# Fixed adjacent pairs of PSUM banks for the exponentials, in place of a pool of single banks, with order rules per stretch to go with them

## The chip, the cores and the metric

One core of a Trainium2 chip. The metric is the device time of one execution in microseconds, the median of several runs; all runs quoted are of the undisturbed state or, for this one-core program, within 1.5% of the fastest of their kernel.

Engines: PE is the TensorE, ACT the ScalarE, DVE the VectorE, POOL the GpSimd.

## The reference, cut

```python
q = (xn @ wq).reshape(B, S, H, Dh)      # S 2048, D 640, H 32 heads of Dh 20
k, v = xn @ wk, xn @ wv                 # one key/value head for all
p = softmax(einsum("bhqd,bkd->bhqk", q, k) * Dh ** -0.5)
attn = einsum("bhqk,bkd->bhqd", p, v).reshape(B, S, H * Dh) @ wo
r = maximum(xn @ w1 + b1, 0)            # F 1536
out = x + attn + (r * r) @ w2 + b2      # xn = layernorm(x)
```

The scores are 32 x 2048 x 2048: 2048 tiles of 128 keys x 512 queries, each an exponential. Most go to ACT; the others are converted on DVE by a bit trick (a scaled integer read as bf16, four weighted copies of it standing for 2^x), in "sets" of four tiles.

## The kernel before

The Python program plans the whole execution first: a greedy planner holds one queue per engine and durations for each operation, picks the next instruction by start time and priority, and only then emits each engine's list with its semaphore waits. Parameters of the planner are overridden per 10 us by RULES. A change of a rule or a bank therefore moves thousands of instructions.

A score visit takes banks for an ACT instruction; this is the part that the change switches (cut):

```python
def make_step():
    j = len(steps)
    if par("STATIC"):
        banks = list(SIDES[j % 2])                  # (0, 1) or (2, 3)
        if any(bank_state(bk) is None for bk in banks):
            return None
        return build_step(j, banks, 0.0)
    t0 = max(free["PE"], horizon() - par("JIT"))
    st_of = {bk: bank_state(bk) for bk in range(NB)}     # NB = 7
    ok = [bk for bk in range(NB) if st_of[bk] is not None and st_of[bk] <= t0 + 0.02]
    if len(ok) >= 3 + par("R3"):                    # three tiles when banks are plenty
        ...
    # else the two adjacent banks that come free first
    ...
def pool_banks():                                   # for DVE tiles and dense units
    if par("STATIC"):
        return [bk for bk in POOLED if bk not in HELD and bank_state(bk) is not None]   # 4, 5, 6
    fb = [bk for bk in POOLED if bank_state(bk) is not None]
    return fb if len(fb) > par("KEEP") else []
```

When a visit is placed, DVE tiles of other heads ride along in it, because row-tiled matmuls of four heads run side by side: in the trace of the kernel before, a visit of two, three or four tiles takes 0.318, 0.321 or 0.325 us until the next group starts.

```python
elif kind == "qk":
    take_step(ap[1])
    heads = [t[2] for t in ap[1]["tiles"]]
    while len(heads) < HPG:                         # HPG = 4
        r = make_dqk(heads)
        ...
        commit(r[0])
        after_dqk(*r)
```

Nearly all other PE work (weighted values, query and key projections, the two dense layers, the output) is column-tiled in groups of four matmuls, most of 512 or 320 columns; the transposes and the value projection use the whole array (128*128 in the views). A unit of the dense layers is a run of such groups into one bank.

The softmax here doesn't subtract the row's maximum and nothing guards it: scores larger than these inputs give would overflow.

Of the kernel before, what the change touches and what calls it, by code (L numbers as in the profile page):

```python
# [24 lines left out]
SCALE = DH ** -0.5  # L25
EPS = 1e-5
EXP_SHIFT = 50.0
# [8 lines left out]
def _pl(z):  # L36
# [9 lines left out]
NB = 7  # L46
PVB = 7
SHARED = (4, 5, 6)
STATIC = False
SIDES = ((0, 1), (2, 3))  # L50
POOLED = tuple(range(NB))
HELD = sum(SIDES, ())
EVP = 0.8
JIT = 0.8
R3 = 2
NOPEN = 2
# [3 lines left out]
DRATE = 0.95  # L60
DLAST = 7.5
DSLACK = 0
URG = 4.0
PBIAS = 0.6
DGAP = 0.5
# [3 lines left out]
WARM = 0.72  # L69
# [7 lines left out]
STG = 10.0  # L77
TAIL0 = 2
ACTEV = (0, 2)
KEEP = 1  # L80
RULES = {3: {'PVA': 2.1, 'PVD': 2.1, 'R3': 1, 'PP': 0.9},
         4: {'PVA': 2.1, 'PVD': 2.1, 'R3': 1, 'PP': 0.9, 'WARM': 0.78},
         5: {'D1P': 1, 'MPRIO': 0.5, 'PBIAS': 2.5},
         6: {'D1P': 1, 'MPRIO': 0.5, 'PBIAS': 2.5, 'ND': 1, 'QKP': 0},
         7: {'DQP': 2.05, 'URG': 2, 'PVD': 2.1, 'BEHIND': -0.3},
         8: {'WARM': 0.85, 'DQP': 0.95},
         10: {'ND': 1, 'NOPEN': 3},
         11: {'ND': 1, 'NOPEN': 3},
         12: {'EPS': 0.12},
         13: {'EPS': 0.06, 'EVP': 0.3},  # L90
         15: {'PBIAS': 0},
         17: {'EPS': 0.06},
         18: {'EPS': 0.12},
         19: {'WARM': 0.78, 'PBIAS': 2.5, 'IDLE': 0.3},
         21: {'PBIAS': 0, 'KEEP': 0},
         23: {'EPS': 0.12},
         25: {'R3': 1, 'EVP': 0.3},
         26: {'R3': 1, 'EVP': 0.3, 'IDLE': 0.3, 'PVD': 2.1},
         28: {'EPS': 0.12, 'URG': 3},
         29: {'EPS': 0.12, 'URG': 3, 'KEEP': 3, 'EVP': 1.1, 'ND': 3},  # L100
         31: {'PBIAS': 1, 'D1P': 1, 'PVD': 1.05},
         32: {'PBIAS': 1, 'D1P': 1, 'PVD': 1.05, 'DGAP': 0.8, 'DQP': 0.95, 'SQP': 2, 'R3': 1},
         36: {'PP': 0.9, 'BEHIND': -0.1, 'EVP': 0.3, 'PBIAS': 1.5},
         37: {'URG': 3, 'JIT': 1.0, 'PVD': 1},
         38: {'SQP': 0.7, 'URG': 3},
         39: {'PP': 2.5},
         40: {'PBIAS': 1},
         41: {'PBIAS': 1, 'DGAP': 1.5, 'SQP': 0.7},
         42: {'PBIAS': 1, 'DGAP': 1.5, 'SQP': 2, 'NOPEN': 3, 'ND': 2, 'PVD': 1},
         43: {'PBIAS': 1, 'DGAP': 1.5, 'SQP': 2, 'NOPEN': 3, 'ND': 2, 'PVD': 1, 'R3': 9},  # L110
         44: {'WARM': 0.78, 'KEEP': 3, 'DLAST': 7.5},
         45: {'DGAP': 0.8, 'KEEP': 1, 'D1P': 3},
         48: {'PBIAS': 1},
         49: {'PBIAS': 1, 'R3': 1},
         50: {'PBIAS': 1, 'R3': 1},
         53: {'DLAST': 3.5},
         54: {'DLAST': 3.5, 'EPS': 0, 'EVP': 0.3},
         55: {'DLAST': 3.5, 'EPS': 0, 'EVP': 0.3, 'ND': 1},
         56: {'EVP': 2, 'MPRIO': 1.0},
         57: {'R3': 1, 'ND': 1},  # L120
         58: {'BEHIND': -0.1, 'EPS': 0, 'PP': 4, 'R3': 1},
         59: {'BEHIND': -0.1, 'EPS': 0, 'PP': 4, 'R3': 1, 'DRATE': 0.95, 'DLAST': 10, 'PVA': 2.1},
         60: {'EVP': 1.1},
         61: {'EVP': 1.1, 'SQP': 0.7},
         62: {'EVP': 1.1, 'SQP': 0.7, 'KEEP': 3, 'R3': 1, 'NOPEN': 2, 'D1P': 3},
         64: {'PP': 0.9, 'DRATE': 0.8},
         65: {'R3': 1},
         66: {'R3': 1},
         67: {'EPS': 0.12, 'PVA': 1.05},
         68: {'R3': 0},  # L130
         69: {'R3': 0, 'JIT': 1.1}}
HOOK = None
PRIO = {'NM15': 2.12, 'NM10': 2.88, 'PW2': 0.96}
NBEF = {'AG4': 10.21, 'NM7': 11.5, 'Qe0_1': 10.11, 'PW12': 25.33}
XACT = (1, 3)
QEACT = (0, 1, 2, 3)
STOP = None
WINDOW = 3.4
MPRIO = 0.9
BEHIND = 0.12  # L140
IDLE = 0.3
EARLY = 12
EARLYK = "F"
FFN0 = 0.3
OUT0 = 0.5
QLEAD = 3.0
PEND = NBLK - 3.0
QCPOS = 0
ACTST = (2, 5, 6)
POOLXN = (2, 7, 9, 10, 11, 13, 14, 15)  # L150
ROWP = (-0.5, 0.6, 0.8, 1.2)


# [3 lines left out]
MODEL = {}  # L157

DEFAULTS = dict(EVP=EVP, PBIAS=PBIAS, MPRIO=MPRIO, DGAP=DGAP, DLAST=DLAST, DRATE=DRATE, BEHIND=BEHIND, IDLE=IDLE, URG=URG, NOPEN=NOPEN,
                EPS=0.03, JIT=JIT, R3=R3, STATIC=STATIC, PVA=1, PVD=1, D1P=1, PP=4, SQP=2, DQP=3, QKP=0, ND=2, WARM=WARM, KEEP=KEEP)  # L160


class Ctr:
# [61 lines left out]
def bass_parallel_sum__grouped_kv_mqa__dense_activation_squared_relu__prompt_kernel(nc, A_x, A_wq, A_wk, A_wv, A_wo, B_x, B_w1, B_b1, B_w2, B_b2, out):  # L225
    es = ExitStack()
    with es:  # L227
# [71 lines left out]
        def one():  # L299
            nsem[0] += 1  # L300
            return newctr(f"d{nsem[0]}")
# [3 lines left out]
        free = {k: 0.0 for k in ENG}  # L305
# [36 lines left out]
        dve_q, pool_q, sp_q, act_q = [], [], [], []  # L342
# [3 lines left out]
        def op(name, eng, dur, fn, deps=(), **kw):  # L346
            o = Op(name, eng, dur, [fn], deps, **kw)
            o.prio = PRIO.get(name, o.prio)
            o.nb = NBEF.get(name, 0.0)
            ev = [d for d in o.deps if isinstance(d, str)]  # L350
            if ev:
                late.setdefault(ev[0], []).append(o)
            else:
                QUE[eng].append(o)
            return o
# [59 lines left out]
        def rows(st):  # L415

            p = ROWP[st // 4]
            if st in ACTST:
                k = ACTST.index(st)
                jk = OC[:, 0, :, :].rearrange("p c n -> p (c n)")[:, k * D:(k + 1) * D] if k < 4 else out_sb[:, k - 4, :]  # L420
# [4 lines left out]
            else:  # L425
# [4 lines left out]
                opm = ALU.subtract  # L430
                if st in POOLXN:
                    s1 = op(f"NM{st}", "DVE", 0.08, lambda e: e.tensor_scalar(out=mv[:, st, 0:1], in0=mv[:, st, 0:1], scalar1=-1.0, scalar2=None, op0=ALU.mult), [ag], prio=p - 0.1)
# [13 lines left out]
        def bank_state(bk):  # L446

            if bank_busy[bk]:
                return None
            o = bank_rel[bk]  # L450
            if o is not None and o.fin is None:
                return None
            return 0.0 if o is None else o.fin + LATS[(o.eng, "PE")]
# [19 lines left out]
        for st in range(4):  # L473
# [17 lines left out]
            k0_op[st] = op(f"KTe0_{st}", "DVE", 0.25, lambda e, cs=cs, kb=kb: e.tensor_scalar(out=kT[:, cs], in0=ps[:, kb, 0:128], scalar1=nk0[:, 1:2], scalar2=None, op0=ALU.add), [km, nk_op], prio=0)  # L491
            if st in QEACT:
                q0_op[st] = op(f"Qe0_{st}", "ACT", 0.25, lambda e, cs=cs, st=st: e.activation(out=qT[:, 0, cs], in_=ps[:, st, 0:128], func=AF.Identity), [qm])
# [24 lines left out]
        def need_k(kt):  # L518
            return [k0_op[kt]] if kt < 4 else [kt_op[kt // 4]]
# [230 lines left out]
        for st in range(0, ST, 2):  # L750
            r0, r1 = 128 * st, 128 * st + 256
            o = op(f"XB{st}", "POOL", 1.25, lambda e, r0=r0, r1=r1: e.dma_start(xbd[r0:r1, :], A_x[0][r0:r1, :], accum_op=ALU.add, max_dma_last_dim=4 * D),
                   [x_b2[st], x_b2[st + 1], HOLD["xb"][st // 2]], lat=12.0, dma=one(), prio=3)
# [22 lines left out]
        left = sum(cost(u) for u, _ in chain)  # L776
        others, t = [], FFN0
        for u, t0 in chain:
# [58 lines left out]
        def next_stage():  # L837
            while free["ACT"] >= stage[0] * STG:
# [3 lines left out]
                now_rules.clear()  # L842
                now_rules.update(RULES.get(stage[0], {}))

        def par(name):

            return now_rules.get(name, DEFAULTS[name])
# [5 lines that stand above are left out]
                banks = list(SIDES[j % 2])  # L853
# [187 lines left out]
        def pool_banks():  # L1041

            if par("STATIC"):
                return [bk for bk in POOLED if bk not in HELD and bank_state(bk) is not None]
            fb = [bk for bk in POOLED if bank_state(bk) is not None]
            return fb if len(fb) > par("KEEP") else []
# [5 lines left out]
        def make_dqk(heads):  # L1052
            opn = [s for s in sets[-NL:] if s["left"]]
            fb = pool_banks()
            if not fb or (len(fb) == 1 and behind()):
                return None
            s = next((s for s in opn if [h for h in s["left"] if h not in heads]), None)
            if s is None:
                if len(opn) >= par("NOPEN"):
                    return None  # L1060
                s = new_set()
                if s is None:
                    return None
            h = [h for h in s["left"] if h not in heads][0]
            b, kt = s["b"], s["kt"]
            deps = need_k(kt) + need_q(b)
            bank = pick_bank(fb)
            deps.append(bank_rel[bank])
            return Op(f"DQK{s['n']}_{h}", "PE", 0.215, [mm(ps[:, bank, :], kT[32 * h:32 * h + DH, kt * 128:(kt + 1) * 128], qT[32 * h:32 * h + DH, b % NQS, :], True, True, (32 * h, 0))],
                      deps, mode="R"), s, h, bank  # L1070
# [121 lines left out]
        while True:  # L1192
# [81 lines left out]
            if pick[2].eng == "PE" and unit[0] is None and fb and pick[0] > free["PE"] + par("IDLE") and pv_begun:  # L1274
                for u in misc[:EARLY]:
                    if u.at > progress() and u.name[0] in EARLYK and u.can():
# [3 lines left out]
                        o = Op(f"{u.name}.0", "PE", dur, ch(), list(u.deps()) + [bank_rel[u.bank]])  # L1280
# [15 lines left out]
            _, prio, o, ap = pick  # L1296
# [162 lines left out]
```

## Time and profile before

| | before |
|---|---|
| time, median | 705.43 us (3 runs), 705.88 with the fourth |
| span of the profile | 703.6 us |
| ACT instructions of exponentials | 665 of two tiles, 50 of three |
| DVE tiles | 568 = 142 sets |
| score visits of PE | 714 |

A "visit" is an unbroken run of score matmuls (out<-in `ps<-qT,kT`) on PE. The visits, and the distances from one start to the next, are counted from the trace; the page has no row for them. The rows that the argument starts from stand in the prediction.

### The profile page before, as it was taken

What the parts mean: (1) busy time and instruction counts of PE and PEld (TensorE: products, weight loads), DVE (VectorE), ACT (ScalarE), POOL (GpSimd) and SP (SyncE); (2) the same over time, 40 slices, a digit from 0 to 9 for tenths busy, and PEclk for the clock granted to TensorE, in tenths of its full rate; (3) what the DMA queues carried; (4) which work ended last, traced back from release to release, by engine and by line L of the source; (5) the groups of instructions that cost most, each with busy time, mean ns of one, the idle gap of its engine ahead of it and who ended that gap; (6) DMA issues with size and microseconds to landing.
All of it is one profiled execution on the core that took longest, in us unless ns stands there. A gap on an engine that the chain in (4) does not pass through costs nothing.

```text
span 703.6 us, 22608 instructions
## 1 busy us (share of the span) xinstructions
PE 695.0 (99%) x9780; PEld 216.0 (31%) x9781; DVE 645.9 (92%) x1125; ACT 687.5 (98%) x739; POOL 427.3 (61%) x268
## 2 busy tenths in 40 slices
PE   8999999999999999999999999999999999999997
PEld 4422223233322223332322222323333222233333
DVE  7789999999999998989998998899899999999894
ACT  6899999999999999999999999999999999999995
POOL 4767556567566764666568765766665675644253
PEclk9999999999999999999999999999999999999999
DMA  6325422233337701211101001111112100031201
GB/s 201 98 70 153 115 78 58 81 97 80 84 85 160 162 20 25 55 40 37 52 18 40 23 22 28 29 47 26 46 42 51 36 22 23 20 106 51 55 26 39
DMA packets 42016, 44.00 MB, mean 63 GB/s; under 512 B 15540, under 2 KB 32772, under 8 KB 41788
## 3 DMA queue, kind: packets, MB, share of 16 engines
q1 hardware_dynamic: 39132, 36.93, 19.2%
q0 software_dynamic: 2208, 5.25, 3.9%
q8 instruction: 76, 1.25, 0.7%
q10 hardware_dynamic: 576, 0.38, 0.2%
q14 instruction: 24, 0.20, 0.1%
HBM read 28.03 MB, written 14.91 MB: 61 GB/s over the span
## 4 chain that ended last, share of the span: by engine, by line
ACT 95%; PE 4%; DMA 1%; DVE 0%; SPq 0%; issue 0%; DVEq 0%
ACT PT L910 94%; PE ps L367 3%; DMA x_sb<-in_A_x_dram 1%; PE ps L540 1%; ACT xnT L477 0%; ACT OC L421 0%; DVE out_sb L1164 0%; PE ps L568 0%; SPq L384 0%; ACT OC L422 0%; SPq L391 0%; PE ps L510 0%; PE ps L496 0%; DVEq L227 0%; DVE PT L1164 0%
## 5 line engine op out<-in xcount | busy, mean ns | idle before, releaser
L910 ACT ACTIVATE PT<-ps 128x1024 bf16<-128x1024 f32 (+1 forms) x715 | 677.1, 1219 | 3.8 <-PE ps L367 3.8
L1083 DVE TENSOR_SCALAR tmore<-ps 128x512 uint16<-128x512 f32 x568 | 367.4, 683 | 31.7 <-PE ps L367 28.2
L1101 POOL TENSOR_SCALAR tmore<-tmore 128x2048 uint16<-128x2048 uint16 x109 | 206.4, 1900 | 171.1 <-PE ps L367 62.3
L367 PE MATMUL ps<-qT,kT 20*128 20x512 bf16 x2048 | 281.7, 384 | 1.9 <-ACT PT L910 0.8
L1101 POOL TENSOR_SCALAR x_sb<-tmore 128x2048 uint16<-128x2048 uint16 x100 | 189.3, 1902 | 79.4 <-DVE x_sb L1101 24.2
L367 PEld LDWEIGHTS ps<-qT,kT 20*128 20x128 bf16 x2048 | 71.6, 91 | 280.4 <-ACT PT L910 233.1
L367 PE MATMUL ps<-PT,vx 128*32 128x512 bf16 x1480 | 136.9, 386 | 0.2 <-ACT PT L910 0.2
L1101 DVE TENSOR_SCALAR x_sb<-tmore 128x2048 uint16<-128x2048 uint16 x135 | 96.1, 745 | 0.1
L367 PE MATMUL ps<-x_sb,vxs 128*32 128x512 bf16 x940 | 83.2, 382 | 0.0
L367 PE MATMUL ps<-xnT,w_sb 128*32 128x512 bf16 x960 | 77.2, 384 | 0.1
L367 PE MATMUL ps<-w_sb,big 128*32 128x320 bf16 x1536 | 74.5, 302 | 0.0
L367 PE MATMUL ps<-tmore,vxs 128*32 128x512 bf16 x764 | 69.6, 382 | 0.0
L1101 DVE TENSOR_SCALAR tmore<-tmore 128x2048 uint16<-128x2048 uint16 x82 | 61.5, 770 | 0.1
L367 PE MATMUL ps<-tmore,vx 128*32 128x512 bf16 x568 | 55.7, 382 | 0.0
L367 PEld LDWEIGHTS ps<-PT,vx 128*32 128x32 bf16 x1480 | 34.9, 94 | 62.1 <-issue 53.6
L367 PEld LDWEIGHTS ps<-w_sb,big 128*32 128x32 bf16 x1536 | 32.1, 95 | 29.3 <-issue 22.2
L648 DVE TENSOR_SCALAR hT_tmp<-ps,b1col 128x512 bf16<-128x512 f32 x48 | 35.8, 746 | 3.4 <-PE ps L367 2.7
L367 PE MATMUL ps<-xnT,wq_sb 128*32 128x512 bf16 (+1 forms) x480 | 33.7, 356 | 0.2 <-DVE tmore L1083 0.2
L367 PE MATMUL ps<-wo_c,OC 128*32 128x320 bf16 x608 | 30.9, 301 | 0.0
L367 PEld LDWEIGHTS ps<-x_sb,vxs 128*32 128x32 bf16 x940 | 21.3, 95 | 19.9 <-issue 13.4
L367 PEld LDWEIGHTS ps<-xnT,w_sb 128*32 128x32 bf16 x960 | 17.6, 94 | 26.7 <-issue 22.4
L367 PEld LDWEIGHTS ps<-tmore,vxs 128*32 128x32 bf16 x764 | 18.1, 95 | 16.4 <-issue 11.5
(81 smaller groups left out, 259.4 us busy)
## 6 DMA issues: line engine op xcount, KB each, us to landing
xbd<-b2d SPq DMA_DIRECT2D x16, 320.0 KB, 4.4
xbd<-in_A_x_dram POOLq DMA_DIRECT2D x8, 640.0 KB, 5.8
xr<-xbd SPq DMA_DIRECT2D x32, 160.0 KB, 2.4
w_sb<-in_B_w_dram SPq DMA_DIRECT2D x8, 480.0 KB, 4.4
big<-OR SPq DMA_DIRECT2D x71, 40.0 KB
big<-drs SPq DMA_DIRECT2D x71, 40.0 KB
out_dram<-out_sb SPq DMA_DIRECT2D x15, 160.0 KB, 1.8
qT<-QCr SPq DMA_DIRECT2D x108, 20.0 KB
```

The source lines that it names most:

```text
L367: return lambda e: e.matmul(out_, l, r, start=start, stop=stop, tile_position=tp)
L540: return [(lambda e, dt=dt: e.transpose(out=psbf(bk)[:, dt * 128:(dt + 1) * 128], in_=xn_sb[:, st, dt:D:DT], identity=ident[:])) for dt in ...
L648: o = Op(f"RL{qc}_{f}", "DVE", 0.66, [lambda e: e.tensor_scalar(out=hT_tmp[:, k % 2, :], in0=ps[:, bk, :], scalar1=b1col[:, f:f + 1], scal ...
L910: return Op(f"ACT{st_['j']}", "ACT", 0.05 + 0.4267 * n, [lambda e: e.activation(out=PT[:, s0:s0 + n, :], in_=ps[:, b0:b0 + (n - 1) * db + ...
L1083: d1 = op(f"D1_{n}_{i}", "DVE", 0.60, lambda e: e.tensor_scalar(out=L[:, cs].bitcast(U16), in0=ps[:, bank, :], scalar1=XA, scalar2=XB, op0 ...
L1101: p = op(f"P{j}_{n}", eng, 0.60 if eng == "DVE" else 1.86, lambda e, T=T, j=j, two=two: e.tensor_scalar(out=T.bitcast(U16), in0=L.bitcast( ...
```

## The change

The intent: give ACT two fixed sides that alternate, so that its supply no longer depends on what the pool has free, leave three banks to everybody else, and choose the rules of all 70 stretches anew for this layout. The durations that the planner uses are the same numbers in both files. The diff, cut:

```diff
-STATIC = False
+STATIC = True
 SIDES = ((0, 1), (2, 3))
...
-KEEP = 1
-RULES = {3: {'PVA': 2.1, 'PVD': 2.1, 'R3': 1, 'PP': 0.9},
...
-         69: {'R3': 0, 'JIT': 1.1}}
+KEEP = 0
+DJIT = 9.0
+RULES = {1: {'EPS': 0.12},
...
+         62: {'NOPEN': 1, 'DGAP': 0.5, 'URG': 3, 'PVD': 1, 'QKP': 1.5},
+         63: {'DGAP': 0, 'PVA': 1.05, 'URG': 2, 'PBIAS': 0},
+         64: {'DGAP': 0.25, 'PVA': 1.05, 'URG': 2, 'PBIAS': 0, 'ND': 3},
+         65: {'DGAP': 0.25, 'PVA': 1.05, 'URG': 2, 'PBIAS': 0, 'ND': 3, 'DQP': 3, 'QKP': 0.97},
...
-QEACT = (0, 1, 2, 3)
+QEACT = (0, 1)
...
-FFN0 = 0.3
+FFN0 = 0.6
...
-ACTST = (2, 5, 6)
-POOLXN = (2, 7, 9, 10, 11, 13, 14, 15)
+ACTST = (0, 2, 4)
+POOLXN = (7, 9, 10, 11, 13, 14, 15)
...
+            if max(free["DVE"], free["PE"]) + sum(o.dur for o in dve_q if o.frees is not None) > free["PE"] + 0.43 + par("DJIT"):
+                return None
```

QKP is the priority of a score visit on PE (lower goes first; 0 by default), MPRIO that of the next group of a dense unit (0.9 by default).

More of the change, by code (lines that the diff above doesn't have):

```diff
@@ L79 @@
 ACTEV = (0, 2)
-KEEP = 1
-RULES = {3: {'PVA': 2.1, 'PVD': 2.1, 'R3': 1, 'PP': 0.9},
-         4: {'PVA': 2.1, 'PVD': 2.1, 'R3': 1, 'PP': 0.9, 'WARM': 0.78},
-         5: {'D1P': 1, 'MPRIO': 0.5, 'PBIAS': 2.5},
-         6: {'D1P': 1, 'MPRIO': 0.5, 'PBIAS': 2.5, 'ND': 1, 'QKP': 0},
-         7: {'DQP': 2.05, 'URG': 2, 'PVD': 2.1, 'BEHIND': -0.3},
-         8: {'WARM': 0.85, 'DQP': 0.95},
-         10: {'ND': 1, 'NOPEN': 3},
-         11: {'ND': 1, 'NOPEN': 3},
-         12: {'EPS': 0.12},
-         13: {'EPS': 0.06, 'EVP': 0.3},
-         15: {'PBIAS': 0},
-         17: {'EPS': 0.06},
-         18: {'EPS': 0.12},
-         19: {'WARM': 0.78, 'PBIAS': 2.5, 'IDLE': 0.3},
-         21: {'PBIAS': 0, 'KEEP': 0},
-         23: {'EPS': 0.12},
-         25: {'R3': 1, 'EVP': 0.3},
-         26: {'R3': 1, 'EVP': 0.3, 'IDLE': 0.3, 'PVD': 2.1},
-         28: {'EPS': 0.12, 'URG': 3},
-         29: {'EPS': 0.12, 'URG': 3, 'KEEP': 3, 'EVP': 1.1, 'ND': 3},
-         31: {'PBIAS': 1, 'D1P': 1, 'PVD': 1.05},
-         32: {'PBIAS': 1, 'D1P': 1, 'PVD': 1.05, 'DGAP': 0.8, 'DQP': 0.95, 'SQP': 2, 'R3': 1},
-         36: {'PP': 0.9, 'BEHIND': -0.1, 'EVP': 0.3, 'PBIAS': 1.5},
-         37: {'URG': 3, 'JIT': 1.0, 'PVD': 1},
-         38: {'SQP': 0.7, 'URG': 3},
-         39: {'PP': 2.5},
-         40: {'PBIAS': 1},
-         41: {'PBIAS': 1, 'DGAP': 1.5, 'SQP': 0.7},
-         42: {'PBIAS': 1, 'DGAP': 1.5, 'SQP': 2, 'NOPEN': 3, 'ND': 2, 'PVD': 1},
-         43: {'PBIAS': 1, 'DGAP': 1.5, 'SQP': 2, 'NOPEN': 3, 'ND': 2, 'PVD': 1, 'R3': 9},
-         44: {'WARM': 0.78, 'KEEP': 3, 'DLAST': 7.5},
-         45: {'DGAP': 0.8, 'KEEP': 1, 'D1P': 3},
-         48: {'PBIAS': 1},
-         49: {'PBIAS': 1, 'R3': 1},
-         50: {'PBIAS': 1, 'R3': 1},
-         53: {'DLAST': 3.5},
-         54: {'DLAST': 3.5, 'EPS': 0, 'EVP': 0.3},
-         55: {'DLAST': 3.5, 'EPS': 0, 'EVP': 0.3, 'ND': 1},
-         56: {'EVP': 2, 'MPRIO': 1.0},
-         57: {'R3': 1, 'ND': 1},
-         58: {'BEHIND': -0.1, 'EPS': 0, 'PP': 4, 'R3': 1},
-         59: {'BEHIND': -0.1, 'EPS': 0, 'PP': 4, 'R3': 1, 'DRATE': 0.95, 'DLAST': 10, 'PVA': 2.1},
-         60: {'EVP': 1.1},
-         61: {'EVP': 1.1, 'SQP': 0.7},
-         62: {'EVP': 1.1, 'SQP': 0.7, 'KEEP': 3, 'R3': 1, 'NOPEN': 2, 'D1P': 3},
-         64: {'PP': 0.9, 'DRATE': 0.8},
-         65: {'R3': 1},
-         66: {'R3': 1},
-         67: {'EPS': 0.12, 'PVA': 1.05},
-         68: {'R3': 0},
-         69: {'R3': 0, 'JIT': 1.1}}
@@ new lines @@
+KEEP = 0
+DJIT = 9.0
+RULES = {1: {'EPS': 0.12},
+         2: {'DGAP': 0.8, 'QKP': 1.5},
+         3: {'DGAP': 0.8, 'QKP': 0.97},
+         5: {'DQP': 0.95, 'PBIAS': 1.5},
+         6: {'DQP': 0.95, 'PBIAS': 1.5},
+         7: {'DLAST': 4.5, 'SQP': 0.7, 'DRATE': 1.1, 'BEHIND': -0.3},
+         8: {'DLAST': 4.5, 'SQP': 0.7, 'DRATE': 1.1, 'BEHIND': -0.3},
+         10: {'PVD': 2.1},
+         12: {'PBIAS': 0.3, 'IDLE': 0.2, 'BEHIND': 0.05},
+         13: {'PBIAS': 0.3, 'IDLE': 0.2, 'BEHIND': 0.05, 'ND': 3, 'NOPEN': 3},
+         14: {'PBIAS': 0.3, 'IDLE': 0.2, 'BEHIND': 0.05, 'ND': 3, 'NOPEN': 3, 'DRATE': 0.8, 'EPS': 0.12},
+         16: {'EPS': 0.12},
+         17: {'PVD': 0.95},
+         19: {'DRATE': 0.8, 'EPS': 0.06},
+         20: {'DRATE': 0.8, 'EPS': 0.06, 'EVP': 0.3, 'MPRIO': 1.1},
+         22: {'WARM': 0.78, 'ND': 1, 'DRATE': 1.1},
+         25: {'PP': 2.5, 'SQP': 0.7, 'DQP': 3},
+         26: {'PBIAS': 0, 'WARM': 0.85, 'SQP': 0.7, 'PVD': 1.05},
+         27: {'PBIAS': 0, 'WARM': 0.85, 'SQP': 0.7, 'PVD': 1.05},
+         28: {'PBIAS': 2.5, 'WARM': 0.85, 'SQP': 0.7, 'PVD': 1.05, 'D1P': 3, 'URG': 3, 'EVP': 0.3},
+         29: {'PBIAS': 2.5, 'WARM': 0.85, 'SQP': 0.7, 'PVD': 1.05, 'D1P': 3, 'URG': 3, 'EVP': 0.3, 'IDLE': 0.1, 'EPS': 0.12, 'DLAST': 7.5},
+         30: {'DQP': 0.95, 'PBIAS': 0.6},
+         31: {'EPS': 0.06},
+         32: {'EPS': 0.06, 'DGAP': 0.5, 'D1P': 0.5, 'PP': 0.9},
+         34: {'DLAST': 3.5, 'DGAP': 0.5},
+         35: {'PP': 0.9, 'SQP': 2},
+         36: {'MPRIO': 0.9, 'PBIAS': 2.5, 'PVD': 1, 'DLAST': 7.5},
+         37: {'MPRIO': 0.9, 'PBIAS': 2.5, 'PVD': 1, 'DLAST': 3.5, 'EVP': 2, 'D1P': 3},
+         39: {'D1P': 1, 'SQP': 0.7, 'URG': 4, 'PBIAS': 2.5},
+         40: {'D1P': 1, 'SQP': 0.7, 'URG': 4, 'PBIAS': 2.5, 'NOPEN': 1},
+         41: {'ND': 1},
+         42: {'ND': 1, 'EPS': 0.12, 'SQP': 0.7, 'D1P': 1},
+         43: {'ND': 1, 'EPS': 0.12, 'SQP': 0.7, 'D1P': 1},
+         44: {'ND': 1, 'EPS': 0.12, 'SQP': 0.7, 'D1P': 1, 'PVA': 1.05, 'NOPEN': 2},
+         45: {'ND': 1, 'EPS': 0.12, 'SQP': 0.7, 'D1P': 1, 'PVA': 1.05, 'NOPEN': 2},
+         46: {'ND': 1, 'EPS': 0.06, 'SQP': 0.7, 'D1P': 1, 'PVA': 1.05, 'NOPEN': 2},
+         47: {'DRATE': 0.95, 'MPRIO': 0.5, 'WARM': 0.72, 'D1P': 0.5},
+         48: {'DRATE': 0.95, 'MPRIO': 0.5, 'WARM': 0.72, 'D1P': 0.5},
+         49: {'DRATE': 0.95, 'MPRIO': 0.5, 'WARM': 0.72, 'D1P': 0.5, 'ND': 1, 'DQP': 2.05},
+         51: {'PP': 2.5},
+         52: {'PP': 2.5, 'EPS': 0.06},
+         53: {'PP': 2.5, 'EPS': 0.06, 'D1P': 3, 'DRATE': 0.95},
+         54: {'PP': 2.5, 'EPS': 0.06, 'D1P': 3, 'DRATE': 0.95, 'MPRIO': 1.0, 'EVP': 1.1, 'PVA': 0.95, 'DQP': 0.95},
+         55: {'URG': 2, 'MPRIO': 1.0, 'QKP': 0.97},
+         58: {'PVA': 1.05},
+         59: {'DLAST': 8.5, 'WARM': 0.78, 'PP': 0.9},
+         60: {'NOPEN': 2, 'DGAP': 0.5, 'URG': 3},
+         61: {'NOPEN': 1, 'DGAP': 0.5, 'URG': 3, 'PVD': 1},
+         62: {'NOPEN': 1, 'DGAP': 0.5, 'URG': 3, 'PVD': 1, 'QKP': 1.5},
+         63: {'DGAP': 0, 'PVA': 1.05, 'URG': 2, 'PBIAS': 0},
+         64: {'DGAP': 0.25, 'PVA': 1.05, 'URG': 2, 'PBIAS': 0, 'ND': 3},
+         65: {'DGAP': 0.25, 'PVA': 1.05, 'URG': 2, 'PBIAS': 0, 'ND': 3, 'DQP': 3, 'QKP': 0.97},
+         68: {'DLAST': 5.5, 'MPRIO': 1.0},
+         69: {'DLAST': 5.5, 'MPRIO': 1.0},
+         70: {'QKP': 0.97, 'DQP': 3, 'MPRIO': 0.9}}
@@ L132 @@
 HOOK = None
-PRIO = {'NM15': 2.12, 'NM10': 2.88, 'PW2': 0.96}
-NBEF = {'AG4': 10.21, 'NM7': 11.5, 'Qe0_1': 10.11, 'PW12': 25.33}
+PRIO = {'XN1': 0.13}
+NBEF = {'S4a': 6.0, 'AG5': 10.23, 'PW1': 4.94}
 XACT = (1, 3)
-QEACT = (0, 1, 2, 3)
+QEACT = (0, 1)
 STOP = None
@@ L159 @@
 DEFAULTS = dict(EVP=EVP, PBIAS=PBIAS, MPRIO=MPRIO, DGAP=DGAP, DLAST=DLAST, DRATE=DRATE, BEHIND=BEHIND, IDLE=IDLE, URG=URG, NOPEN=NOPEN,
-                EPS=0.03, JIT=JIT, R3=R3, STATIC=STATIC, PVA=1, PVD=1, D1P=1, PP=4, SQP=2, DQP=3, QKP=0, ND=2, WARM=WARM, KEEP=KEEP)
+                EPS=0.03, JIT=JIT, R3=R3, STATIC=STATIC, PVA=1, PVD=1, D1P=1, PP=4, SQP=2, DQP=3, QKP=0, ND=2, WARM=WARM, KEEP=KEEP, DJIT=DJIT)
 class Ctr:
```

## The prediction

> **What bounds the kernel now.** First the head of the page and the chain of work that ended last.
>
> ```profile
> PE 695.0 (99%) x9780; PEld 216.0 (31%) x9781; DVE 645.9 (92%) x1125; ACT 687.5 (98%) x739; POOL 427.3 (61%) x268
> ...
> ACT 95%; PE 4%; DMA 1%; DVE 0%; SPq 0%; issue 0%; DVEq 0%
> ACT PT L910 94%; PE ps L367 3%; DMA x_sb<-in_A_x_dram 1%; PE ps L540 1%; ACT xnT L477 0%; ACT OC L421 0%; DVE out_sb L1164 0%; PE ps L568 0%; SPq L384 0%; ACT OC L422 0%; SPq L391 0%; PE ps L510 0%; PE ps L496 0%; DVEq L227 0%; DVE PT L1164 0%
> ```
>
> The chain says ScalarE (ACT): its exponentials (L910) fill 94% of the span. But PE is busy 99% too, so the chain, which follows one engine, does not settle which of the two is the limit. Next, the groups by shape: how the score tiles (128x512 each, 2048 in all) are shared out.
>
> ```profile
> L910 ACT ACTIVATE PT<-ps 128x1024 bf16<-128x1024 f32 x665 | 621.9, 1190 | 1.4 <-PE ps L367 1.4
> L910 ACT ACTIVATE PT<-ps 128x1536 bf16<-128x1536 f32 x50 | 79.0, 1609 | 2.3 <-PE ps L367 2.3
> ...
> L1083 DVE TENSOR_SCALAR tmore<-ps 128x512 uint16<-128x512 f32 x568 | 367.4, 683 | 31.7 <-PE ps L367 28.2
> ...
> L367 PE MATMUL ps<-qT,kT 20*128 20x512 bf16 x2048 | 281.7, 384 | 1.9 <-ACT PT L910 0.8
> ```
>
> 665x2 + 50x3 = 1480 tiles go through ACT in 715 instructions; 568 tiles go through VectorE (DVE), which is 142 sets of four. The mean durations (1190, 1609) overlap their neighbours, so I took start-to-start distances from the trace: a two-tile instruction follows at 0.904 us (its median and its tenth percentile), a three-tile one at 1.330. 665x0.904 + 50x1.330 = 667.7 us. The first starts at 15.30 and the last ends at 695.14, 679.8 later: 12 us more than the floor, of which 3 lie in two waits before 33 us (0.5 and 2.5) and some 8.6 are hundreds of delays too short to show as idle. After the last there are 8.5 us of tail.
>
> Now PE, in the timeline from 420 to 424 us:
>
> ```profile
> 420.77 0.61 PE L367 MATMUL ps<-xnT,wq_sb 128*32 128x512 bf16 x8
> ...
> 421.32 0.39 PE L367 MATMUL ps<-qT,kT 20*128 20x512 bf16 x3
> ...
> 421.64 0.40 PE L367 MATMUL ps<-xnT,wq_sb 128*32 128x512 bf16 x4
> ...
> 421.87 0.39 PE L367 MATMUL ps<-PT,vx 128*32 128x512 bf16 x4
> ...
> 422.19 0.39 PE L367 MATMUL ps<-qT,kT 20*128 20x512 bf16 x2
> 422.50 0.12 PEld L367 LDWEIGHTS ps<-xnT,w_sb 128*32 128x32 bf16 x8 [0.23 <-issue]
> 422.51 0.62 PE L367 MATMUL ps<-xnT,w_sb 128*32 128x512 bf16 x8
> ```
>
> The score matmuls split the array by rows, all others by columns. From scores to others the next start comes 0.32 us later, from others to others 0.22-0.23, from others back to scores 0.32. So a visit to the scores costs about 0.322 + 0.105 = 0.427 us, whether it makes two, three or four tiles. I grouped the trace's matmuls so: 714 visits for 715 ACT instructions, i.e. nearly every DVE tile rides along in a visit that ACT needs anyway. Set against these floors (0.216 and 0.321 for 512 columns, 0.136 and 0.241 for 320, 0.318 after scores), PE loses only 8.5 us to waits over 13 ns between 33 and 690 us. PE is therefore as full as ACT: two bounds at once, PE 1.3% from its floor and ACT about 1.3%. Only 3 filler groups (x12 matmuls on zeros) are left to drop.
>
> DVE's conversions follow each other at 0.60 us; its idle time is spread in waits on PE (28.2 us in the row above). It is third, and POOL fourth.
>
> **What the Trainium skill says.** "TensorEngine Tiling (Array Packing)", Key Properties: changing the tiling mode drains the TensorE. The trace agrees: 0.32 against 0.22 us, with the loads' 0.23 us of "issue" at each change. "Perfetto Trace Analysis", Identifying the Most-Contended Engine: matmul busy share is no measure of distance to the limit; use the busy share of weight loads. Here that misleads: loads are busy 31% while the start distances leave PE hardly any room. "ScalarE: Activation LUTs", Rules for kernel authors: some 0.3 us per ACTIVATE plus 0.83 ns per element. The second half agrees ((1.330-0.904)/512 = 0.83 ns); back to back the first does not: 0.904 - 2x0.426 = 0.05 us. "PSUM — Partial Sum Buffer", PSUM bank collisions: two engines must not use one bank and quadrant at once; hence a bank is given on only after its reader is done, which is why the shape of the bank pool decides when a visit can start.
>
> **The change part by part.**
> (1) With the pool, an ACT instruction takes two adjacent free banks of seven, or three when five are free. After, instruction j takes banks (0,1) or (2,3) in turn and never three; DVE tiles and the units of the dense layers share banks 4 to 6. With 142 sets, 1480 tiles need 740 instructions. ACT: 740x0.904 = 669.0, +1.3 us. PE: 740 - 714 = 26 more visits x 0.427 = +11.1 us. This is the main term: ACT's cost of narrow instructions is small, PE's is not.
> (2) More or fewer sets. One set more takes four tiles off ACT (-1.81 us) and two visits and one PV group off PE (-0.85 - 0.22), and adds four weighted groups (4x0.22 = +0.88): -0.19 us for PE. Five sets more are -9 us for ACT but only -1.0 for PE. DVE has room for some (a set is 4x0.60 plus 1.5 passes of 0.60 = 3.3 us), so ACT can be relieved and PE cannot.
> (3) Banks: three for DVE and units. A unit holds one about half of the time (100 units x some 3 us / 700); a DVE tile holds one for two visits, about 1.8 us. 2.5/1.8 = 1.4 tiles per us against 0.86 needed (568/660). No bound. Each ACT side is refilled in 0.21 + 0.22 + 0.22 us of hand-overs and matmul (estimate from the kernel's constants, consistent with the timeline), less than the other side's 0.904, but with only some 0.25 us to spare, about one PE group. With PE at 0.93 us per step (672/724) this is tolerable.
> (4) Start. Two query evictions move from ACT to DVE, one normalisation from POOL to DVE, and ACT takes the statistics of rows 0, 2, 4. The 2.5 us wait at 29.7 us ends on a key chunk (matmuls 29.63, eviction 30.94, scores 32.00), so on the order of the first stage, not on banks. I allow -1.5 us.
> (5) Rules per 10 us. They move work inside queues; they can take back waits but no work. Of PE's 8.5 us I allow -4, since ACT, with sets to spare, no longer binds together with PE. The new DVE backlog limit of 9 us is above any wait seen in this trace and should do nothing.
>
> Sum: 705.4 + 11.1 - 1.0 - 1.5 - 4 + about 0 of tail = 710; I round towards the rivals below and say 709.
>
> **Rivals.**
> A: the fixed pairs and reordered stretches win a little, 698-704. For it: rules chosen for this layout, removable delays of 8.6 us on ACT and 2.5 in the start. Against: PE's visits are arithmetic, and no ordering removes them. One chance in four.
> B: fewer sets as well as narrower instructions, because DVE gets three banks and no loan from seven. With 130 sets ACT needs 764x0.904 = 691 + 15 + 3 + 6 + 8.5 = 723 and becomes the bound alone. Against: bank arithmetic in (3). One in twelve.
> C: two sides leave ACT waiting whenever a PE group straddles its release; 0.02 us in each of 740 steps is +15 us on ACT. It would show above all if ACT still bound; with PE at 0.93 per step most of it is hidden. It is what could carry 709 to 716.
>
> **Range and chances.** The visits alone give 716 if nothing is regained, everything regained gives 700 (716.5 - 8.5 - 3 - several sets and tail). So 700 to 718. A gain over 2% means under 691.3 and would need PE at less than its floor: 0.02. A loss over 2% means over 719.5 and needs rival B or a bad C: 0.07. Within 2%: 0.91.
>
> **What would show it right or wrong.** Right: no 1536-wide rows, 725-740 of 1024; score visits 725-745 at an unchanged 0.32; PE at its floor with waits of 4-9 us; small idle time before L910 and chain shares moved from ACT towards PE. Part (2) is wrong if the DVE tiles are below 560 or above 620. Part (4) is wrong if the first exponential is not near 15 us and ACT's first 50 us are no fuller. The main term is wrong if the visits rise by 20 or more and the time does not rise: then PE had slack that I read as work, or the tail and start gave more than allowed.

## More of the kernel before

One more view, the chain of work that ended last in order of time (start, duration, what), of the kernel before:

```profile
32.44 661.79 ACT PT L910 x699
694.23 0.04 issue
694.27 3.90 PE ps L367 x104
```

From 32 us on, one unbroken run of ACT's exponentials, then a short tail of PE.

## The result, and the profile after

711.86 us (711.78 to 711.92, 4 runs) against 705.88 (4 runs): ratio 1.0084, 95% interval 1.0067 to 1.0102. Ratios here are the mean time of one kernel's fast runs over that of the other's of the same rounds, so not quite the ratio of the medians quoted. The change costs 6 us, within 2%.

Head of the page of the kernel after and its chain by line; then two groups by shape from the page (busy us, mean ns, idle before them):

```profile
PE 703.1 (99%) x9789; PEld 216.2 (30%) x9789; DVE 649.0 (91%) x1127; ACT 688.1 (97%) x760; POOL 440.9 (62%) x275
...
ACT 74%; PE 24%; DVE 0%; DMA 0%; issue 0%; POOL 0%
...
L915 ACT ACTIVATE PT<-ps 128x1024 bf16<-128x1024 f32 x738 | 678.3, 1186 | 10.6 <-PE ps L372 10.6
L1090 DVE TENSOR_SCALAR tmore<-ps 128x512 uint16<-128x512 f32 x572 | 369.4, 681 | 30.9 <-PE ps L372 26.8
```

ACT's busy time has hardly moved (687.5 to 688.1), PE's has grown by 8.1 us. The three-tile exponentials are gone, there is one DVE set more (143), and ACT's visible idle time before exponentials rose from 3.8 to 10.6 us. A fifth of the chain has gone from ACT (95 to 74%) to PE (4 to 24%). The chain in order of time says where:

```profile
38.18 245.78 ACT PT L915 x268
283.96 0.05 issue
284.01 63.35 PE ps L372 x898
347.36 0.02 issue
347.38 269.62 ACT PT L915 x294
617.00 0.05 issue
617.05 82.77 PE ps L372 x1310
```

After 617 us the chain is PE's matmuls to the end. ACT's busy time by stretch, before and then after (stretch and its length, busy us and instructions, granted clock, DMA share, GB/s):

```profile
550.00:600.00 50.00, 50.00 (x55) 1.00 0.11 27
600.00:650.00 50.00, 50.00 (x54) 1.00 0.20 61
650.00:690.00 40.00, 40.00 (x38) 1.00 0.13 36
```

```profile
550.00:600.00 50.00, 50.00 (x56) 1.00 0.16 41
600.00:650.00 50.00, 47.13 (x52) 1.00 0.18 53
650.00:690.00 40.00, 36.71 (x41) 1.00 0.16 45
```

Up to 600 us the two kernels are as far with the attention as each other: counted in the traces, 1273 and 1272 ACT tiles, 504 and 505 DVE tiles. But before has done 374 of 395 groups of the first dense layer and the query and key projections, after only 350 (all that is missing is of the dense layer); both have done the same 368 groups of 320 columns. 24 x 0.216 = 5.2 us of PE work has been put off, and after 600 us it is paid. What took its place is mostly visits: by 600 us the kernel after has made 631, before 622, and 9 x 0.427 = 3.8 us. This is what paying looks like, in the timeline of the kernel after:

```profile
649.52 1.80 PE L372 MATMUL ps<-w_sb,big 128*32 128x320 bf16 x48
...
651.15 0.85 PE L372 MATMUL ps<-wo_c,OC 128*32 128x320 bf16 x20
651.94 0.12 PEld L372 LDWEIGHTS ps<-qT,kT 20*128 20x128 bf16 x6 [0.26 <-issue]
651.94 0.61 PE L372 MATMUL ps<-qT,kT 20*128 20x512 bf16 x6
...
652.37 1.94 ACT L915 ACTIVATE PT<-ps 128x1024 bf16<-128x1024 f32 x2 [1.61 <-PE ps L372]
```

A whole output unit (17 groups) runs without a break, ACT goes dry for 1.6 us, and then one visit of six matmuls fills both sides at once.

Where the 6 us come from, in PE's own terms. The priced terms of PE's time, from the traces:

| | before | after | difference in us |
|---|---|---|---|
| score visits (x 0.427) | 714 | 727 | +5.6 |
| weighted-value groups (x 0.22): of ACT tiles, of DVE sets | 370, 568 | 369, 572 | +0.7 |
| filler groups (x 0.216) | 3 | 1 | -0.4 |
| waits over 13 ns, 33 us to the end | 9.3 | 9.7 | +0.3 |
| score matmuls that follow score matmuls in one visit | 3.2 us | 3.4 us | +0.2 |
| sum | | | +6.4 |

The span grew by 6.6, the time by 6.0. Waits are counted here from 33 us to the end; between 33 and 690 us, as in the prediction, they are 8.5 before and 9.3 after. The sum is an account from counts: no run adds or removes just these 13 visits.

### The profile page after: what moved, and what is told of

Its sections match the earlier page's. It is cut to its first block, busy times and chain, and to the rows that moved or that the text cites. A ratio compares the mean times of both kernels' runs of the same rounds, so it can differ in the third digit from the quotient of the medians.

```text
span 710.2 us, 22598 instructions
## 1 busy us (share of the span) xinstructions
PE 703.1 (99%) x9789; PEld 216.2 (30%) x9789; DVE 649.0 (91%) x1127; ACT 688.1 (97%) x760; POOL 440.9 (62%) x275
## 4 chain that ended last, share of the span: by engine, by line
ACT 74%; PE 24%; DVE 0%; DMA 0%; issue 0%; POOL 0%
ACT PT L915 74%; PE ps L372 23%; DMA x_sb<-in_A_x_dram 0%; PE ps L515 0%; PE ps L480 0%; PE ps L573 0%; DVE OR L431 0%; PE ps L501 0%; PE ps L545 0%; DVE OR L432 0%; POOL rstd L439 0%; DVE PT L1171 0%; DVE big L441 0%; DVE mv L433 0%; DVE mv L434 0%
## 5 line engine op out<-in xcount | busy, mean ns | idle before, releaser
L915 ACT ACTIVATE PT<-ps 128x1024 bf16<-128x1024 f32 x738 | 678.3, 1186 | 10.6 <-PE ps L372 10.6
L1108 POOL TENSOR_SCALAR tmore<-tmore 128x2048 uint16<-128x2048 uint16 x114 | 215.9, 1906 | 137.8 <-PE ps L372 39.7
L372 PE MATMUL ps<-qT,kT 20*128 20x512 bf16 x2048 | 287.3, 384 | 1.5 <-ACT PT L915 1.0
L1108 POOL TENSOR_SCALAR x_sb<-tmore 128x2048 uint16<-128x2048 uint16 x103 | 194.5, 1899 | 102.9 <-PE ps L372 61.3
L372 PE MATMUL ps<-w_sb,big 128*32 128x320 bf16 x1536 | 76.4, 302 | 0.0
L372 PE MATMUL ps<-xnT,w_sb 128*32 128x512 bf16 x960 | 75.2, 384 | 0.0
L1108 DVE TENSOR_SCALAR tmore<-tmore 128x2048 uint16<-128x2048 uint16 x78 | 58.2, 765 | 0.0
L661 DVE TENSOR_TENSOR big<-hT_tmp 128x512 bf16<-128x512 bf16 x48 | 23.4, 498 | 0.1
```

What stands on the lines that cost most here:

```text
L372: return lambda e: e.matmul(out_, l, r, start=start, stop=stop, tile_position=tp)
L661: q = op(f"SQ{qc}_{f}", "DVE", 0.34, lambda e: e.tensor_tensor(out=h2T[:, f, :], in0=hT_tmp[:, k % 2, :], in1=hT_tmp[:, k % 2, :], op=ALU. ...
L915: return Op(f"ACT{st_['j']}", "ACT", 0.05 + 0.4267 * n, [lambda e: e.activation(out=PT[:, s0:s0 + n, :], in_=ps[:, b0:b0 + (n - 1) * db + ...
L1108: p = op(f"P{j}_{n}", eng, 0.60 if eng == "DVE" else 1.86, lambda e, T=T, j=j, two=two: e.tensor_scalar(out=T.bitcast(U16), in0=L.bitcast( ...
```

## The experiments

Theory 1: PE's work sets the time; the pairs cost because they need more score visits, each of 0.427 us, and the order only chooses where that is paid. Rivals: theory 2, the rules are what differs; theory 3, the banks, by fewer DVE sets or by waits of ACT; and that the late stalls of ACT are themselves the loss. Twelve runs; before had medians of 705.73, 705.66 and 705.48 in them, and the kernel after was not timed again, so it stands at its 711.86 us. Several kernels freeze the planned order and edit it just before emission, since a planner that plans anew answers any disturbance with another order.

**1 to 4. Banks without chosen rules.** Rules off; in the second run three-tile instructions are forbidden, in the third the kernel after pools its banks again.

```diff
-        now_rules.update(RULES.get(stage[0], {}))
+        now_rules.update({})
-R3 = 2
+R3 = 99            # pooled_norules_pairs only
-STATIC = True
+STATIC = False     # pairs_norules_pooled only
```

> The kernel before with its rules per 10 us switched off (defaults throughout). Counted in the built program: 140 DVE sets, 731 ACT instructions (26 of three tiles), 722 visits of PE to the scores. Theory 1 (PE's work sets the time, a visit costs 0.427 us): 8 more visits than before are 3.4 us, two sets fewer add 0.4 us of PE, the rest of any loss are waits that the rules had removed: 709 to 716. Theory 2 (the choice of rules is what separates the kernels of before and after, the banks are not): this one loses as much as the pairs without rules do, or more.

> As the run above, but three-tile instructions forbidden, banks still pooled: 140 sets, 744 instructions of two tiles, 742 visits. Theory 1: 20 more visits than the run above x 0.427 = +8.5 us, less what waits absorb: +4 to +9. A theory in which ACT is the bound gives 744x0.904 - (705x0.904 + 26x1.330) = +0.7 us only.

> The kernel after with its rules off and the banks pooled again (its other settings kept): 139 sets, 738 instructions (16 of three tiles), 730 visits. Theory 1: within 4 us of the pooled kernel without rules (8 visits more, 3.4 us). Theory 2: the same as the next run within 2 us.

> The kernel after with its rules off: 136 sets, 752 instructions of two tiles, 743 visits. Against the run above only the banks differ. Theory 1: 13 visits x 0.427 + 3 sets x 0.19 = +6.1 us. Theory 3 (three fixed banks for DVE and the units give fewer sets, and ACT becomes the bound): 752x0.904 - (722x0.904 + 16x1.330) = +5.8 us, with ACT's excess over its floor unchanged and PE's waits grown. The two are told apart by PE's waits: no more than 10 us in theory 1, 15 or more in theory 3. Theory 2: no difference beyond 2 us.

| | sets | ACT instr. | visits | filler groups | waits | scores after scores, us | time |
|---|---|---|---|---|---|---|---|
| before | 142 | 715 | 714 | 3 | 9.3 | 3.2 | 705.73 |
| pooled_norules | 140 | 731 | 722 | 8 | 10.0 | 9.8 | 716.26 |
| pooled_norules_pairs | 140 | 744 | 742 | 8 | 10.7 | 4.9 | 718.86 |
| pairs_norules_pooled | 139 | 738 | 730 | 13 | 9.8 | 9.0 | 718.81 |
| pairs_norules | 136 | 752 | 743 | 31 | 9.8 | 6.0 | 724.82 |

Without rules the fixed pairs cost 6.0 us against the pool with the same settings (718.81 to 724.82), as much as with chosen rules, so theory 2 falls: the rules are worth 10.5 us to the pool and 13 to the pairs, on top of a difference that the banks make. The 6.0 us contain the ban on three tiles (the pooled kernel made 16 such instructions). The other settings of the change (queue orders, KEEP, the backlog limit DJIT and so on) make up the step from 716.26 to 718.81, 2.5 us; none of them was tested alone. Forbidding three tiles in the pool cost 2.6 us, less than the +4 to +9 expected: 20 visits are 8.5 us, but 4.9 us of scores that follow scores in one visit went away (where they wait for a bank, the column's time is waiting). For the last run the mark set beforehand, PE's waits of no more than 10 us against 15 or more, came out for theory 1 (9.8), but it is not pure theory 1 either: three sets fewer (-2.0 us of weighted values), and 18 filler groups more (+3.9 us), which the planner sets only where PE would idle. So without rules theory 3 has a share, fixed banks give fewer sets and an idler PE; the chosen rules had brought the sets back to 143 and the fillers to 1. The same sum as in the table above gives 10.4, 4.3 and 4.5 us for the steps of 10.5, 2.6 and 6.0: right to within 2 us, not better.

**5 and 6. What a visit costs.** Order frozen; at 25 places the riding DVE tiles go behind the next column group.

```diff
+        for ride, c in [cand[i * len(cand) // N] for i in range(N)]:    # N = 25, 60 to 600 us
+            for o in ride:
+                order_all.remove(o)
+            i = order_all.index(c) + 1
+            order_all[i:i] = ride
```

> The kernel after with its order frozen, but at 25 places spread from 60 to 600 us the DVE tiles that rode along in a score visit are moved behind the next column-tiled group: the same work in 25 more visits. Theory 1 (PE full, a visit costs 0.427 us): +8 to +10.7 us (25 x 0.427). If a visit costs only the matmul it holds, or PE has slack: 0 to +3.

> The same 25 splits in the kernel before. Theory 1: +8 to +10.7 us as well, since its PE is as full. If the kernel before is bound by ACT alone, clearly less than in the kernel after: under +5.

717.49 and 711.42 us, +5.6 (over the 711.86) and +5.8, with exactly 25 visits more in each trace (752, 739). That is less than the 8 to 10.7 expected. PE's waits between 33 and 690 us fell in both, from 9.3 to 4.4 and from 8.5 to 4.2: 10.7 - 4.9 = 5.8 and 10.7 - 4.3 = 6.4. So the work of 25 visits is there at 0.427 us each, and waits took up almost half. Net, a visit added to a frozen order cost 0.23 us, and 13 at that price would be 3 us. In the kernel after, PE's waits did not fall against before, so the account above charges its 13 visits in full; why they did not fall is not tested. The kernel before loses as much as the kernel after, so its PE is as full.

**7 and 8. Relief of PE alone, of ACT alone**, in the kernel after, order frozen; both change the result (the narrowed one stays inside the tolerance).

```diff
+        for o in [o for o in order_all if o.name.startswith("FFN") and o.name.endswith(".2")]:    # pairs_less48
+            order_all.remove(o)
-            ... e.activation(out=PT[:, s0:s0 + n, :], in_=ps[:, b0:b0 + (n - 1) * db + 1:db, :], ...
+            ... e.activation(out=PT[:, s0:s0 + n, 0:480], in_=ps[:, b0:b0 + (n - 1) * db + 1:db, 0:480], ...    # pairs_narrow
```

(pairs_narrow also fills the columns left out with ones, once, on POOL.)

> Wrong result on purpose: the kernel after, order frozen, without one of the five matmul groups of each of the 48 units of the first dense layer: 48 x 0.216 = 10.4 us less PE work, ACT's work untouched. Theory 1: the stalls of ACT where PE catches up (some 8 us between 600 and 655 us) shrink, so -2 to -6 us; not the whole 10.4, because the order is that of the full work and ACT then binds in the middle. If ACT or the banks are the bound: 0 to -1.

> Wrong result on purpose: the kernel after, order frozen, each exponential over 480 of 512 columns, so each of 738 instructions is 2 x 32 x 0.83 ns = 0.053 us shorter: 39 us less ACT work, PE's work untouched. Theory 1: the time falls by no more than PE's own waits on ACT, some 9 us. If ACT is the bound: -25 to -39 us.

39 us less of ACT work gave 8.4 us (703.43): who waits for whom on PE's weight loads (total us, times, longest), after and then narrowed.

```profile
PEld ps L372 <- ACT PT L915: 284.6, 711, 0.7
PEld ps L372 <- issue: 158.1, 689, 0.4
```

```profile
PEld ps L372 <- issue: 254.0, 961, 0.4
PEld ps L372 <- ACT PT L915: 176.2, 431, 0.4
```

These rows are not waits alone: their sum hardly falls (442.7 to 430.2 us), because the time at each change of tiling (0.23 us "issue" in the prediction's timeline) stands in them too, and moves from ACT's row to "issue". By the floors of the prediction, the true waits over 13 ns fell from 9.3 to 1.6 us. PE is then at its floor at 703 us, and still 31% of weight loads.

10.4 us less of PE work gave 0.2 us (711.62), where 2 to 6 were expected: theory 1, as I had put it, failed this test. The page says where the work went:

```profile
PE 698.3 (98%) x9597; PEld 214.5 (30%) x9597; DVE 648.7 (91%) x1127; ACT 688.2 (97%) x760; POOL 440.6 (62%) x275
```

PE is 4.8 us less busy and waits instead: 19.4 us between 33 and 690 where it was 9.3. (The profiled execution was the slowest of the five, 713.1 us; its first exponential came at 16.20 us instead of 14.53, so the difference lies in the start.) The late stalls from 641 to 655 us stand as they were, 1.10, 0.48, 1.73 and 1.78 us: the groups taken out lie before them. In the middle ACT runs at its own floor (0.904 us per instruction, mostly 0.6 to 0.9 us of excess per 50 us), and with the order frozen PE cannot use the room to do later work earlier. So PE is not the only bound: in the middle it and ACT are locked together, and only what is planned into that room counts. Theory 1 corrected: the time is set by PE's work as long as the order is planned to fill PE.

**9 and 10. The two kernels with ACT out of the way, and both reliefs together.**

> Wrong result on purpose: the narrowing of the run pairs_narrow (480 of 512 columns per exponential) in the kernel before, order frozen. PE's floor of the kernel before then shows. Theory 1: -6 to -8 us against before (its waits of some 9 us vanish but for 1 to 2), so 698 to 700, and the two kernels keep their distance of 5 to 6 us with ACT out of the way: the 13 visits. If the distance was a matter of ACT or of bank hand-overs to ACT, the two narrowed kernels come within 2 us of each other.

> Wrong result on purpose: pairs_narrow and the 48 groups of pairs_less48 taken out together. The relief of PE alone gave -0.2 us, that of ACT alone -8.4. Theory 1 as corrected (in the middle PE and ACT are locked together at ACT's 0.904 us, PE is next to bind): with ACT out of the way PE's relief counts in full, -9 to -10.4 us against pairs_narrow, 693 to 694.5. If something third (DVE, banks) holds the narrowed kernel at 703: 0 to -3.

The kernel before, narrowed: 697.18 us, with a scatter (695.86 to 702.54) that the other kernels don't have; its ratio to before is 0.9894, that of pairs_narrow 0.9968, and the difference, 0.74%, is 5.2 us (6.2 between the medians). With the 95% intervals of the two ratios (0.9852 to 0.9935, 0.9956 to 0.9981) this leaves some 2 to 8 us, just clear of the "within 2 us" of the rival. PE's waits there are 2.1 us to the end. The pages of the two narrowed kernels, first the one made from before, then the one made from after:

```profile
PE 686.4 (99%) x9780; PEld 214.9 (31%) x9781; DVE 645.8 (93%) x1125; ACT 667.3 (96%) x739; POOL 427.7 (62%) x269
...
PE 96%; DVE 1%; ACT 1%; DMA 1%; SPq 0%; issue 0%; DVEq 0%
```

```profile
PE 695.5 (99%) x9789; PEld 216.7 (31%) x9789; DVE 647.9 (92%) x1127; ACT 667.6 (95%) x760; POOL 440.7 (63%) x276
...
PE 94%; DVE 2%; POOL 2%; DMA 1%; SPq 0%; ACT 0%; issue 0%
```

The chain is PE's in both, ACT is as busy in one as in the other, and PE is 9.1 us busier in the second. So the distance of the two kernels remains when ACT is not in the way: it is in PE's work, not in the supply of ACT. This is the run that weighs most.

Both reliefs: 698.47, 5.0 us below pairs_narrow. The 9 to 10.4 expected did not come; 0 to 3 did not either. Relief of PE counts once ACT is out of the way, but only half. The traces place the rest: from 33 us to the end PE's waits rose from 1.8 us to 4.0, and its scores that follow scores, now without a group between them, from 2.5 to 5.8; 10.4 - 2.2 - 3.3 = 4.9. In a fixed order part of any relief turns into waits for the next dependence.

**11. Relief of PE where ACT stalls late.** 32 groups of four output units out.

```diff
+        for o in [o for o in order_all if any(o.name == "OUT%d.%d" % (n, k) for n in (16, 17, 18, 19) for k in range(2, 10))]:
+            order_all.remove(o)
```

> Wrong result on purpose: the kernel after, order frozen, without 8 of the 17 matmul groups of four output units that stand where ACT stalls late (640 to 655 us): 32 x 0.136 = 4.4 us less PE work there and nowhere else. Theory 1: -3 to -4.4 us, the late stalls shorter by as much (48 groups all over the kernel gave 0.2). If the late stalls are of ACT's bank hand-over: 0 to -1.

711.34 us, -0.5: not the 3 to 4.4 expected. The stalls of 1.73 and 1.79 us over the floor did shrink to 0.93 and 0.98, but new ones came (0.96, 0.39), and PE waited for DVE's passes. From its timeline:

```profile
651.36 0.10 PEld L372 LDWEIGHTS ps<-x_sb,vxs 128*32 128x32 bf16 x4 [0.42 <-DVE x_sb L1108]
...
655.45 0.40 PE L372 MATMUL ps<-tmore,vxs 128*32 128x512 bf16 x4 [0.69 <-DVE tmore L1108]
```

The visits around the removed groups merged as well, 723 instead of 727. The account is then 4.4 us of groups and 4 x 0.427 = 1.7 us of visits less, against 5.5 us more of waits and of scores that follow scores (the two together, counted again from the traces, 12.9 and 18.4): 0.6. The run rules out nothing: a stall that PE's units make does shrink with them, but in a frozen order the gain turns into waits, some of them for DVE.

**12. The rule that makes ACT wait, removed**; order planned anew.

```diff
-         62: {'NOPEN': 1, 'DGAP': 0.5, 'URG': 3, 'PVD': 1, 'QKP': 1.5},
+         62: {'NOPEN': 1, 'DGAP': 0.5, 'URG': 3, 'PVD': 1},
-         65: {..., 'ND': 3, 'DQP': 3, 'QKP': 0.97},
+         65: {..., 'ND': 3, 'DQP': 3},
```

> The kernel after without the rule that in two late stretches (stages 62 and 65) puts the dense layers' matmuls ahead of the scores; order planned anew. Counted in the built program: 142 sets, 740 instructions, 733 visits. Theory 1 (the late stalls pay a debt of PE work, they are not the loss): the stalls of ACT between 600 and 655 us go, the last exponential ends 4 to 7 us earlier, and the dense work is left behind it: no gain, +0 to +4 us. Rival (the stalls that the rule makes are the loss): -4 to -7 us.

714.66 us, +2.8: as theory 1 said. The chain in order of time, and ACT's busy time by stretch:

```profile
347.33 298.95 ACT PT L915 x326
646.27 0.05 issue
646.32 63.78 PE ps L372 x1150
```

```profile
600.00:650.00 50.00, 50.00 (x56) 1.00 0.17 50
650.00:690.00 40.00, 40.00 (x45) 1.00 0.12 31
```

No stall between 600 and 690 is left, and the last exponential ends at 695.8 us, as in the kernel before (695.1). But the last instruction of an engine ends 14.9 us after it, where in the kernel after it is 6.3: the dense layers' work stands behind. So the stalls after 600 us are how the work put off is done, not the loss itself, and the rule that makes them was worth 2.8 us. Nearly all of that is visits again: 733 instead of 727, 6 x 0.427 = 2.6 us, since fewer stalls let fewer instructions share a visit.

None of the runs that do the full work points to a version faster than the kernel before, whose layout already has the fewest visits of those tried.

## Why the prediction was right

It said 709 us, 700 to 718, within 2%; the time is 711.86. By its steps:

- **Two bounds at once, PE 1.3% from its floor.** Right: 25 visits more cost the kernel before 5.8 us, and 39 us less of ACT work gave the kernel after 8.4. What I had not said is that with two engines so locked, relief of PE alone is nearly worthless in a fixed order (0.2 us for 10.4), and relief of ACT alone gives a fifth (8.4 us for 39).
- **The visits, +11.1 us.** The mechanism was right, the count was off: 13 more, not 26, so +5.6. Two of the missing 13 are the two instructions that the 143rd set saves. The other eleven: I took one visit per ACT instruction; 738 instructions needed 727 visits. Counting instructions less visits in the trace (net of the few visits that hold DVE tiles alone), the eleven lie thus: 5 in the first 100 us, none from 100 to 600, 6 after. Those are the stretches where ACT had run dry, both sides were free, and one visit filled both, as at 651.94 us above. The term priced a steady state and missed that stalls give visits back; with the late stalls gone (pairs_noqkp) 740 instructions needed 733.
- **More sets, -1.0 us.** One set more, not five, so nearly nothing of the 1.0 us came.
- **Start, -1.5 us.** The first exponential came 0.8 us earlier (14.53), the waits of the first 50 us stayed: 2.9 us over ACT's floor against 3.2. The lead of three tiles at 50 us is two at 150 (292 to 290) and gone at 350 (726 to 727).
- **Waits regained by chosen rules, -4 us.** Wrong: PE's waits went from 9.3 to 9.7. The step that failed is the reason given, that ACT "no longer binds together with PE": in the middle it still does, with one set to spare and not five, and there 10.4 us less of PE work gained 0.2.
- **Rivals.** A (a win, one in four) didn't happen, as PE's visits did rise; but that no ordering removes visits was too strong, since stalls merged eleven. B happens only without rules: 136 sets there, 143 with them. C, ACT waiting at bank hand-overs, isn't seen: from 100 to 600 us ACT's excess over its floor is 0.56 to 0.73 us per 50 us in most stretches of both kernels, 1.13 in one. (The prediction's 0.93 us per step is what came: 687.1 us for 738 instructions; its 672 and 724 stand in no trace. Nor does any run here test the page's rule on PSUM bank collisions that it names.)

Two errors of about 5 us (13 visits too many, 4 us of waits not regained) stood against each other, so that 709 came so near to 711.86 is in part luck. The range held because it allowed for each error.

## What to carry to other kernels

Where two tilings of the PE alternate, count the changes, not the matmuls: in these traces a change costs nearly the same for two tiles or four (0.318 and 0.325 us), so anything that makes a batch narrower is paid in changes. When two engines are full and the planner favours one, the work that the other puts off can show much later as stalls of the favoured one (here, groups of 320 columns stood at 130 against 147 already at 300 us, and ACT stalled after 617); compare the work done by a given time in both kernels before you believe the stall. And test such a kernel with its order frozen, but a frozen relief that gives nothing can mean "locked", and does not show "not the bound".

## What the Trainium skill lacked or had wrong

- "TensorEngine Tiling (Array Packing)", Key Properties, says that a change of tiling mode drains the engine, and gives no figure: here some 0.10 us each way (0.321 against 0.216 from a 512-column group to scores; 0.318 from scores to others, where a second batch of scores in one visit adds 0.216), 0.427 us for a visit of two to four score tiles, and 25 such visits added 5.6 and 5.8 us net.
- "Perfetto Trace Analysis", Identifying the Most-Contended Engine, would judge PE by MFU (not worked out here) and the busy share of weight loads: the latter is 31% in the narrowed kernel, whose PE waits 1.6 us in 657. With tilings that alternate, distances from start to start are needed.
- "TensorE: Matmul & The Clock Gate", Back-to-back issue gap, gives some 131 ns as the sustained spacing of 512-column matmuls and about 216 ns for the isolated one, and says nothing there of column-tiled groups. Such groups of four here never came closer than 0.215 us, and nearly all lie at 0.216 or 0.226: the isolated figure, for four matmuls at once.
- "ScalarE: Activation LUTs", Rules for kernel authors: the 0.83 ns per element holds (0.904 and 1.330 us for 1024 and 1536 columns); the 0.3 us per ACTIVATE agrees with the duration of one (1190 ns for 1024 columns, some 0.34 us over the elements), but in an unbroken stream only 0.05 us of it is seen from start to start. The page says elsewhere that instructions back to back overlap, by some 93 ns; here it is some 0.29 us.
- No page has the point that when two engines are saturated together, 10.4 us of work less on one of them gave 0.2 us in an unchanged order.
